# Seven products for half of the first expert's inner width on two thirds of the tokens

## The chip, the cores and the metric

One core of a Trainium2 chip runs the whole program in one launch. The time is the device time of one execution in microseconds (us), as a median over runs. The engines are TensorE (PE, with its weight loads as PEld), VectorE (DVE), ScalarE (ACT), GpSimd (POOL) and SyncE (SP), which issues nearly all DMAs.

## What is computed

Three layers follow each other on 2304 tokens of width 512. Attention of the linear kind comes first, then a mixture of four experts with dense gates, then a two-layer network with an ELU:

```python
# 4 batches x 8 heads, 576 tokens, head width 64
q_s = exp(q - max_d q); q_s /= sum_d q_s
k_s = exp(k - max_s k); k_s /= sum_s k_s
x = q_s @ (k_s^T @ v)                     # -> 2304 tokens x 512
p = probs / probs.sum(-1)
y = sum over e in 0..3 of p[:, e] * (relu(x @ w1[e]) @ w2[e])     # inner width 1024 each
h = y @ w_in                              # inner width 2048, weights in float64
out = where(h > 0, h, exp(min(h, 0)) - 1) @ w_out
```

## The kernel before

**Number format.** Each float32 operand of a matmul is kept as two parts, a high one rounded for the PE and a low one (the rest). A product then takes three matmuls: high by high, low by high, high by low. Every value that PE writes therefore costs one ACT instruction (the high part) and one DVE or POOL instruction (the low part).

**Plain stage.** Expert 0 goes by plain products. The tokens are cut into `blocks`: seven of 256 and one of 512. The inner width of 1024 is cut into 8 parts of 128 (`FPU = 8`, index f). For every (block, f) `first` calls `hidden` (12 matmuls: 4 of depth by 3), has ACT write the relu's high part (L1440) and DVE its low part (L1441), and then `second` does the 12 matmuls of the (block, f) before this one (L1408 does all plain matmuls). So the order on PE is hidden(k), second(k-1), hidden(k+1), second(k).

**Seven products.** All later work goes in steps (s, b): s counts slices of 4 parts (512) of inner width, b the three groups of 768 tokens. Both layers of a step are a 2 by 2 block product that is done by seven products instead of eight (`PRODUCTS`, `SECOND`), with sums and differences of the quarters made beforehand on DVE and POOL. A step has 84 matmuls of 384 columns for the first layer (L1578) and 84 for the second (L1788 in the experts, L1701 in the last network), which are done in between the products of the next step. The slice s = `S_MOE` is the first of the last network: there the tokens are the experts' sums, and their quarters are split on the spot (`own_steps`, L1346 and L1354).

**Side work.** While PE does the plain stage, the other engines prepare what comes later. `at(n, fn)` hangs a piece of work on hook n; a hook falls due after every 2048 columns of plain matmuls (`HOOK`), which is 24 hooks for a block of 256 tokens with 8 parts. Hung there are:

- the attention of the 12 pairs of heads whose tokens come later (`plan_k`, `plan_q`; names like `qmax`, `ksub`, `kvlo`, with L564, L579, L485, L610, L632, L552, L462 on DVE). Batch i / 4 must be done before the block that holds its first token.
- `spread(b)` for the three groups of tokens: the sums T1 to T4 of the quarters of x and their two parts, L953 (two inputs in SBUF, 128 x 768) and L959 (low part), each on DVE or on POOL as the table `MOVES` says, then stored to DRAM for the seven products.
- eight of the 32 pieces of `convert`, which turn the float64 weights of the last network into float32 with integer operations on DVE (L710, L716, L720, L726, L729). The other 24 lie in the steps.
- the gates (`normalise`, `p_turn`, `p_scale` with L903) and the weights of the first step (`w1_steps`).

In the steps `at2` does the same with 24 hooks a step. `MOVES` holds some hundreds of numbers that shift single pieces from their hook or name their engine (`'d'` DVE, `'p'` POOL). Each engine works through its instructions in the order in which they were written down; nothing is reordered on the chip.

## Time and profile before

| | |
|---|---|
| median of 3 runs | 1157.36 us (1156.95 to 1158.04) |
| the profiled execution | 1158.24 us, of which the span of its instructions is 1156.5 us |
| PE busy | 1139.9 us, 99% |
| DVE busy | 959.2 us, 83% |
| POOL busy | 665.2 us, 58% |
| ACT busy | 655.7 us, 57% |
| HBM | 230 GB/s over the span |

The profile comes from one execution. Busy time of an engine is the time in which at least one of its instructions is under way. A matmul's shown duration includes its way through the array, so PE counts as busy also where the next matmul starts long before the last has ended; how fast PE goes is read from the distance of the starts.

### The profile page before, as it was taken

Reading aid. Unit: us, or ns where it says so; the run is one execution under the profiler, and the core shown is the slowest. Engines: PE = TensorE matmul, PEld = TensorE weight load, DVE = VectorE, ACT = ScalarE, POOL = GpSimd, SP = SyncE. Lnnn points to the kernel's source line nnn. Section 1 sums busy time; section 2 is a strip of 40 time slices with the busy share of each in tenths; the row PEclk is TensorE's granted clock in tenths of the full one; section 3 lists DMA queues with packets and bytes.
Section 4 is the critical chain, followed back from the end, with each engine's and each line's share of the span. In section 5 each row is a group of like instructions: output and inputs, shape, how many; then the busy total and the mean of one; then the engine's idle time right before and its main releaser. Section 6 shows DMA issues by size and latency. Waiting matters only on the chain. (4 is left out here: it accounts for less than half of the span.)

```text
span 1156.5 us, 20274 instructions
## 1 busy us (share of the span) xinstructions
PE 1139.9 (99%) x7198; PEld 1117.8 (97%) x7198; DVE 959.2 (83%) x1538; ACT 655.7 (57%) x1386; POOL 665.2 (58%) x567
## 2 busy tenths in 40 slices
PE   8999999999999999999999999999899999999998
PEld 7999999989999999999999999998899999999998
DVE  8977877766788888899899988989787979879976
ACT  6554543335455455455445445456798767767763
POOL 4523445326567567567666655666687547645643
PEclk9999999999999999999999999999999999999999
DMA  9556555876677776777877887814777564665463
GB/s 275 151 144 215 176 193 191 308 251 250 246 255 264 271 261 257 271 269 262 284 274 241 303 266 259 284 68 159 275 242 266 200 231 173 230 230 205 174 247 109
DMA packets 125241, 266.77 MB, mean 231 GB/s; under 512 B 12428, under 2 KB 50004, under 8 KB 125140
## 3 DMA queue, kind: packets, MB, share of 16 engines
q1 hardware_dynamic: 122900, 262.33, 65.6%
q10 hardware_dynamic: 2240, 3.15, 0.8%
q8 instruction: 57, 0.93, 0.3%
q14 instruction: 44, 0.36, 0.1%
HBM read 218.21 MB, written 47.22 MB: 230 GB/s over the span
## 5 line engine op out<-in xcount | busy, mean ns | idle before, releaser
L1578 PE MATMUL m<-xh,w1s 128*128 128x384 f32 x840 | 245.0, 337 | 5.5 <-DVE half L1632 2.9
L1578 PE MATMUL h<-xh,w1s 128*128 128x384 f32 x840 | 243.7, 336 | 1.8 <-DVE half L1632 1.1
L1578 PEld LDWEIGHTS m<-xh,w1s 128*128 128x128 f32 x840 | 154.3, 188 | 9.9 <-DVE half L1632 3.2
L1578 PEld LDWEIGHTS h<-xh,w1s 128*128 128x128 f32 x840 | 154.3, 188 | 5.1 <-DVE m L1871 1.8
L1578 PE MATMUL m<-xl,w1s 128*128 128x384 f32 x420 | 140.7, 335 | 0.0
L1578 PE MATMUL h<-xl,w1s 128*128 128x384 f32 x420 | 140.4, 334 | 0.0
L1408 PE MATMUL o<-hpa,w2t 128*128 128x256 f32 (+1 forms) x768 | 119.3, 300 | 1.0 <-DVE hpa L1441 0.8
L1408 PE MATMUL h<-xh,w1t 128*128 128x256 f32 (+1 forms) x512 | 111.3, 296 | 0.0
L1408 PEld LDWEIGHTS o<-hpa,w2t 128*128 128x128 f32 x768 | 103.9, 191 | 5.7 <-DVE hpa L1441 1.4
L1816 POOL TENSOR_TENSOR accs<-part,accs 128x768 f32<-128x768 f32 x35 | 67.6, 1932 | 68.8 <-DVE part L1815 60.9
L1788 PE MATMUL o<-xh,w2g 128*128 128x384 f32 x432 | 95.2, 334 | 0.0
L1788 PE MATMUL o<-hpa,w2g 128*128 128x384 f32 x432 | 93.7, 334 | 0.0
L1788 PE MATMUL o<-xl,w2g 128*128 128x384 f32 x432 | 93.4, 335 | 0.0
L1408 PEld LDWEIGHTS h<-xh,w1t 128*128 128x128 f32 x512 | 85.6, 191 | 2.5
L1121 POOL TENSOR_TENSOR w2g<-r,w2g 128x512 fp32r<-128x512 f32 x56 | 80.9, 1453 | 12.2 <-ACT w2g L1120 12.2
L1578 PEld LDWEIGHTS m<-xl,w1s 128*128 128x128 f32 x420 | 78.9, 188 | 0.2
L1578 PEld LDWEIGHTS h<-xl,w1s 128*128 128x128 f32 x420 | 78.9, 188 | 0.0
L1408 PE MATMUL h<-xl,w1t 128*128 128x256 f32 (+1 forms) x256 | 77.0, 301 | 0.5 <-DVE xl L632 0.5
L1788 PEld LDWEIGHTS o<-xl,w2g 128*128 128x128 f32 x432 | 76.4, 188 | 0.5 <-ACT o L1798 0.3
L1788 PEld LDWEIGHTS o<-xh,w2g 128*128 128x128 f32 x432 | 76.6, 188 | 0.1
L1788 PEld LDWEIGHTS o<-hpa,w2g 128*128 128x128 f32 x432 | 76.6, 188 | 0.0
L1714 DVE TENSOR_TENSOR accs<-o,accs 128x768 f32<-128x768 f32 (+1 forms) x69 | 62.6, 908 | 4.3 <-PE o L1701 4.3
(366 smaller groups left out, 2899.6 us busy)
## 6 DMA issues: line engine op xcount, KB each, us to landing
xh<-xs SPq DMA_DIRECT2D x189, 384.0 KB, 6.1
xl<-xs SPq DMA_DIRECT2D x189, 384.0 KB, 6.5
xs<-xh SPq DMA_DIRECT2D x42, 384.0 KB, 3.9
xs<-xl SPq DMA_DIRECT2D x42, 384.0 KB, 4.0
r<-in_w_dram SPq DMA_DIRECT2D x56, 256.0 KB, 3.9
extra<-prow SPq DMA_DIRECT2D x38, 192.0 KB, 5.8
x<-in_w_in_dram SPq DMA_DIRECT2D x12, 512.0 KB, 5.1
x<-in_w_out_dram SPq DMA_DIRECT2D x12, 512.0 KB, 6.1
```

What stands on the lines that cost most here:

```text
L1121: eng_of(nc.gpsimd, "w2lo", cls(s), op).tensor_tensor(out=t[:, 1], in0=src, in1=t[:, 0].bitcast(F32), op=ALU.subtract)
L1408: nc.tensor.matmul(out, lhsT, rhs, **kw)
L1578: nc.tensor.matmul(dst, t[:, wl, c + dl, :], x[xl_][:, dl, :], start=(n == 0 and p < 2), stop=(n == 5), skip_group_check=True,)
L1714: nc.vector.tensor_tensor(out=a, in0=x, in1=a, op=ALU.add)
L1788: nc.tensor.matmul(o[:, m], l, r, start=(k < 2 and n == 0), stop=(n == 5), skip_group_check=True)
L1816: nc.gpsimd.tensor_tensor(out=a, in0=r, in1=a, op=ALU.add)
```

## The change

Expert 0's inner width is halved by way of doing it: f = 0 to 3 stay plain for all tokens. f = 4 to 7 stay plain for the first three blocks (`FULL = 3`, 768 tokens) only; for the tokens from 768 on they become a new slice s = 0 of the seven products, with the steps (0, 1) and (0, 2) (`STEP0 = 1` leaves out the step (0, 0)). All later slices move up by one. The plain stage has 144 hooks instead of 216, so the attention of the last 12 pairs starts in a closer rhythm (`K_START`: every 7 hooks instead of every 11), the three `spread` start 20 and 26 hooks apart and go one piece a hook (36 apart and one piece every second hook before), the gates go early, and six of the eight conversions of the plain stage go into the steps (six for each spell of three steps in the second and third spell, instead of four). `spread` keeps its running sums in `gt` instead of a pool's tile, and puts T1 to T4 into other quarters. The table `MOVES` has new numbers nearly throughout, by which also single sums and low parts change between DVE and POOL.

```diff
@@ -22,209 +22,267 @@
...
+    ('spe', 1, 1): 'd', ('spe', 1, 10): 'd', ('spe', 1, 12): 'd', ('spe', 1, 13): 'p',
...
@@ -275,7 +333,7 @@
-    K_START = [8, 13, 20, 29] + [40 + 11 * n for n in range(8)]
+    K_START = [8, 13, 20, 29] + [38 + 7 * n for n in range(8)]
...
-    STEPS = [(s, b) for s in range((NU - 1) * FPU // FS) for b in range(NB)]
-    S_MOE = (E - 1) * FPU // FS
+    STEPS = [(s, b) for s in range((NU * FPU - FS) // FS) for b in range(NB)]
+    STEP0 = 1
+    FULL = 2 * TB // 256
+    S_MOE = (E * FPU - FS) // FS
...
         def new(n):
-            r = stg.tile([P, 2, DM], F32, tag="r", name="sum")
-            t[n] = r[:, :, :TB]
+            k = "ab".index(n)
+            t[n] = gt[:, 2 * k : 2 * k + 2]
...
-            u, c = divmod(FPU + s * FS + f, FPU)
+            u, c = divmod(FS + s * FS + f, FPU)
...
     for b in range(NB):
         need = min(NP_, -(-2 * TB * (b + 1) // S) * NPAIR)
-        t = 66 + 36 * b
+        t = (66, 86, 112)[b]
...
-            at(t + 2 * n, grd(b, n, fn, need), "sprd", b, n)
...
+            at(t + n * (1, 1, 1)[b], grd(b, n, fn, need), "sprd", b, n)
...
-    CONV = [(at, t, 1 + (t < 100), True) for t in (30, 50, 70, 146, 160, 173, 185, 197)]
+    CONV = [(at, t, 1 + (t < 100), True) for t in (30, 50)]
     SPELL = NB * SH
     CONV += [
         (later, SPELL * n + t, d, False)
         for n in range(S_FAST)
-        for t, d in (((10, 2), (34, 1), (48, 1), (62, 1)) if n < 3 else ((6, 1), (20, 1), (34, 1), (48, 1), (62, 1)))
-        if (n, t) != (0, 10)
+        for t, d in (((59, 1),) if n == 0 else ((20, 1), (34, 1), (48, 1), (62, 1)) if n == 5 else
+                     ((6, 1), (18, 1), (30, 1), (42, 1), (54, 1), (66, 1)) if n < 3 else
+                     ((6, 1), (20, 1), (34, 1), (48, 1), (62, 1)))
     ]
...
+    def parts_in(bi):
+        return FPU if bi < FULL else FS
+
     def hidden(u, bi, fs, d0, d1):
...
-    steps = [(0, bi, (f,)) for bi in range(len(blocks[0])) for f in range(FPU)]
+    steps = [(0, bi, (f,)) for bi in range(len(blocks[0])) for f in range(parts_in(bi))]
...
     for i, (s, b) in enumerate(STEPS):
         moe, fill = s < S_MOE, {}
-        if fast(i - 1):
+        if i < STEP0:
+            continue
+        if i == STEP0:
+            pass
+        elif fast(i - 1):
```

How the order of instructions moves is shown at three places. The first is PE in the fourth block of the plain stage (tokens 768 to 1023), where f = 3 ends; the numbers of the weights' buffers tell the parts apart. Before, w1t_449 is f = 3 and w1t_504 is f = 4:

```order
L1408 MATMUL h_1711<-xh_89,w1t_449 128x256
L1408 MATMUL o_1653<-hpa_92,w2t_433 128x256 x6
L1408 MATMUL o_1654<-hpa_92,w2t_433 128x256 x2
...
L525 MATMUL m_1748<-accs_91,ek_1600 64x65 x10
L1408 MATMUL o_1654<-hpa_92,w2t_433 128x256 x4
L1408 MATMUL h_1772<-xh_89,w1t_504 128x256
```

In the changed kernel w1t_326 is f = 3 and w1t_320 is f = 0:

```order
L1491 MATMUL h_1834<-xh_89,w1t_326 128x256
L1491 MATMUL o_1752<-hpa_92,w2t_325 128x256 x6
L1491 MATMUL o_1753<-hpa_92,w2t_325 128x256 x2
...
L655 MATMUL m_1870<-ident_81,accs_91 128x96 x6
L539 MATMUL m_1878<-gx0_93 128x128
L1491 MATMUL o_1753<-hpa_92,w2t_325 128x256 x4
L1491 MATMUL h_1888<-xh_89,w1t_320 128x256
```

After f = 3 the next block begins, where f = 4 followed.

The second place is DVE between two relus of that stage (L1441 before, L1527 in the changed kernel, the same instruction). Before, from the 28th relu to the 29th and on:

```order
L1441 SCALAR_TENSOR_TENSOR hpa<-h,hpa 128x256
L953 TENSOR_TENSOR sum<-sum,xl 128x2x384
L564 TENSOR_REDUCE qm<-accs 96x12
L1441 SCALAR_TENSOR_TENSOR hpa<-h,hpa 128x256
L485 TENSOR_TENSOR ek<-m,ek 128x640
L610 TENSOR_TENSOR ql<-m,qh 128x576
L726 SCALAR_TENSOR_TENSOR ce<-gt,ce 128x512
L1441 SCALAR_TENSOR_TENSOR hpa<-h,hpa 128x256
```

In the changed kernel, in the block of tokens 1024 to 1279 (L1027 is L953, L1033 is L959, L692 is L632, L630 is L570, L612 is L552):

```order
L1527 SCALAR_TENSOR_TENSOR hpa<-h,hpa 128x256
L692 TENSOR_TENSOR xl<-m,xh 128x576
L1027 TENSOR_TENSOR gt<-xh 128x768
L554 TENSOR_SCALAR ks<-m 128x1
L555 RECIPROCAL ks<-ks 128x1
L1027 TENSOR_TENSOR gt<-gt,xl 128x768
L630 TENSOR_TENSOR accs<-accs,qm 96x768
L612 SCALAR_TENSOR_TENSOR kvs<-m,ks,kvs 64x64 x2
L1527 SCALAR_TENSOR_TENSOR hpa<-h,hpa 128x256
```

Where two or three larger instructions stood between two relus, five stand now.

The third place is POOL in the same stretch. Before (L587 and L570 are the two products and differences on q, L474 a memset):

```order
L953 TENSOR_TENSOR sum<-xh 128x2x384
L474 MEMSET gx_93 128x128
L570 TENSOR_TENSOR accs<-accs,qm 96x768
L953 TENSOR_TENSOR sum<-sum,xl 128x2x384
L587 TENSOR_TENSOR accs<-accs,qs 96x768
L474 MEMSET accs 128x128
L959 TENSOR_TENSOR xl<-sum,xh 128x2x384
```

In the changed kernel (L647 is L587):

```order
L647 TENSOR_TENSOR accs<-accs,qs 96x768
L534 MEMSET accs 128x128
L1027 TENSOR_TENSOR gt<-gt,xl 128x768
L1027 TENSOR_TENSOR gt<-xh,gt 128x768
L1027 TENSOR_TENSOR gt<-gt,xl 128x768
L534 MEMSET gx0_93 128x128
L1033 TENSOR_TENSOR xl<-gt,xh 128x2x384
L1027 TENSOR_TENSOR gt<-xh,gt 128x768
L1027 TENSOR_TENSOR gt<-gt,xl 128x768
L1033 TENSOR_TENSOR xl<-gt,xh 128x2x384
```

The pieces of `spread` stand closer to each other here, with fewer pieces of the attention between them.

## Rows read from the trace of the kernel before

**Rows 1.** The page: busy time of each engine.

```profile
PE 1139.9 (99%) x7198; PEld 1117.8 (97%) x7198; DVE 959.2 (83%) x1538; ACT 655.7 (57%) x1386; POOL 665.2 (58%) x567
```

**Rows 2.** Stretches: length, busy PE, PEld, DVE, ACT, POOL (instructions), granted clock, DMA.

```profile
40.00:222.00 182.00, 181.96 (x1662) 178.44 (x1661) 139.61 (x253) 84.62 (x175) 71.64 (x52) 1.00 0.61 198
343.00:600.00 257.00, 256.89 (x1476) 255.28 (x1476) 222.68 (x327) 128.57 (x267) 169.92 (x131) 1.00 0.77 267
774.00:815.00 41.00, 34.20 (x184) 31.34 (x183) 39.03 (x59) 29.49 (x59) 29.25 (x23) 1.00 0.40 149
```

**Rows 3.** Timeline of PE: first and last of a hidden's twelve matmuls, twice.

```profile
102.28 0.28 PE L1408 MATMUL h<-xh,w1t 128*128 128x256 f32 x1
...
103.60 0.28 PE L1408 MATMUL h<-xh,w1t 128*128 128x256 f32 x1
...
252.94 0.39 PE L1408 MATMUL h<-xh,w1t 128*128 128x512 f32 x1
...
255.44 0.39 PE L1408 MATMUL h<-xh,w1t 128*128 128x512 f32 x1
```

**Rows 4.** The chain that ended last, one piece: start, length, what.

```profile
848.33 2.08 PE o L1701 x12
```

**Rows 5.** Groups on DVE from 40 to 222 us: busy, mean ns, idle before.

```profile
L1441 DVE SCALAR_TENSOR_TENSOR hpa<-h,hpa 128x256 fp32r<-128x256 f32 x51 | 21.3, 418 | 20.8 <-ACT hpa L1440 20.5
L953 DVE TENSOR_TENSOR sum<-sum,xl 128x768 f32<-128x768 f32 x8 | 12.8, 1596 | 1.1 <-POOL sum L953 1.0
L579 DVE TENSOR_REDUCE qs<-accs 96x12 f32<-96x768 f32 x12 | 11.2, 937 | 1.0 <-ACT accs L574 0.9
L564 DVE TENSOR_REDUCE qm<-accs 96x12 f32<-96x768 f32 x11 | 10.3, 941 | 0.0
...
L632 DVE TENSOR_TENSOR xl<-m,xh 128x576 fp32r<-128x576 f32 x12 | 9.0, 753 | 6.1 <-ACT xh L628 5.9
...
L959 DVE TENSOR_TENSOR xl<-sum,xh 128x768 fp32r<-128x768 f32 x7 | 6.6, 945 | 1.3 <-ACT xh L956 1.2
L720 DVE SCALAR_TENSOR_TENSOR gt<-gt 128x512 f32<-128x512 uint32 x5 | 5.8, 1166 | 0.0
...
L462 DVE TENSOR_REDUCE nm<-gx 128x1 f32<-128x576 f32 x6 | 4.5, 742 | 0.0
L953 DVE TENSOR_TENSOR sum<-xh,sum 128x768 f32<-128x768 f32 x4 | 3.8, 947 | 0.0
...
L953 DVE TENSOR_TENSOR sum<-xh 128x768 f32<-128x768 f32 x3 | 2.8, 947 | 0.0
...
L710 DVE TENSOR_SCALAR ce<-gt 128x512 uint16<-128x512 uint16 x5 | 2.7, 538 | 1.4 <-DMA gt<-in_w_in_dram 1.4
```

**Rows 6.** Instructions by line: least, median and longest ns, first and last start.

```profile
L1441 DVE SCALAR_TENSOR_TENSOR hpa<-h,hpa x64: 357/423/693, 24.4 to 256.6; 128x256 fp32r<-128x256 f32 x56, 128x512 fp32r<-128x512 f32 x8
...
L903 DVE TENSOR_TENSOR accs<-accs,gx x6: 681/950/2597, 224.2 to 254.3; 128x768 f32<-128x768 f32 x5, 128x512 f32<-128x512 f32 x1
```

**Rows 7.** Timeline of DVE, then of POOL, around 174 us.

```profile
174.09 4.02 DVE L953 TENSOR_TENSOR sum<-sum,xl 128x768 f32<-128x768 f32 x1 [1.03 <-POOL sum L953]
178.03 0.41 DVE L1441 SCALAR_TENSOR_TENSOR hpa<-h,hpa 128x256 fp32r<-128x256 f32 x1
...
174.02 1.47 POOL L570 TENSOR_TENSOR accs<-accs,qm 96x768 f32<-96x768 f32 x1
175.45 1.84 POOL L959 TENSOR_TENSOR xl<-sum,xh 128x768 fp32r<-128x768 f32 x1
```

**Rows 8.** Groups on ACT and on POOL from 40 to 222 us.

```profile
L1440 ACT ACTIVATE hpa<-h 128x256 fp32r<-128x256 f32 x51 | 19.4, 380 | 45.6 <-PE h L1408 45.5
...
L953 POOL TENSOR_TENSOR sum<-sum,xl 128x768 f32<-128x768 f32 x10 | 18.6, 1858 | 9.9 <-DVE sum L953 9.6
```

**Rows 9.** PE's longest wait, and the stretch right behind it.

```profile
PE m L1578 <- DVE half L1632: 2.9, 1, 2.9
815.00:826.00 11.00, 11.00 (x57) 11.00 (x56) 6.91 (x10) 7.08 (x15) 5.94 (x5) 0.85 0.74 288
```

125 lines of the change are left out of this document (75 added, 50 removed), and 439 rows, old and new, of the table MOVES.

## The prediction

> **What bounds the kernel now.** The page comes first: PE is busy for 99% of the span, the next engine, DVE, for 83% [rows 1]. A share of 99% does not say how fast PE goes, so the next view is PE's timeline, and there the distance of the starts. In the plain stage the twelve matmuls of a hidden start from 102.28 to 103.60, eleven distances in 1.32 us, 0.120 us for 256 columns; with 512 columns it is 2.50 / 11 = 0.227 us [rows 3]. In the steps the chain shows twelve matmuls of 384 columns in 2.08 us, 0.1733 us each [rows 4]. PE goes at these rates nearly everywhere. The table of stretches gives the exception: from 774 to 815 us, where the slice S_MOE begins, it is idle for 6.8 of 41 us and DVE busy for 39.0 [rows 2]. So time is PE's work, plus the places where DVE can't keep up. In the plain stage it could: 139.6 of 182 us, with PE idle for 0.04 us [rows 2].
>
> **The change, PE's part.** Removed are f = 4 to 7 of blocks 3 to 7 (counted from 0). Four blocks of 256 lose 4 x 4 x 24 = 384 matmuls, 384 x 0.120 = 46.1 us; the block of 512 loses 96, x 0.227 = 21.8 us. Added are two steps of 168 matmuls, 336 x 0.1733 = 58.2 us. PE's work falls by 46.1 + 21.8 - 58.2 = **9.7 us**. The seam between plain stage and first step is the same in both orders, so it costs nothing new.
>
> The rows give 32 columns' worth more per matmul than its own columns at 2.4 GHz (0.120 against 0.107 us), for each size. The Trainium skill, TensorE: Matmul & The Clock Gate, section Back-to-back issue gap, gives a lone matmul N/2.4 + 2.5 ns; by it the three prices would be 0.109, 0.216 and 0.163 us and the gain 8.0 us, as an estimate. The trace's rates differ from it, and the sum goes by the trace.
>
> **DVE in the shorter plain stage.** The attention of 12 pairs and the three spreads have 72 hooks less to hide under. I counted DVE's instructions in the changed order by blocks. The densest are blocks 3 and 4 (tokens 768 to 1279, eight relus): 8 L1441 at 0.418, 5 L953 at 1.293 (the mean over its three rows, (8 x 1.596 + 7 x 0.947) / 15), 4 L959 at 0.945, and three each of L579, L564, L485, L632, L610 and L462, 4.93 us for the six [rows 5]. That is 3.3 + 6.5 + 3.8 + 14.8 = 28.4 us. Another 26 instructions (2 L903 at 0.950 [rows 6], 3 L570, 1 L587, 8 L552 and 12 small ones of the same view) make 10.1 us. Instructions that follow at once overlap: the relu of 178.03 starts 0.08 us before the one of 174.09 ends [rows 7]; 61 x 0.08 = 4.9 us. DVE needs 38.5 - 4.9 = **33.6 us** there.
>
> PE needs 8 x 24 x 0.120 = 23.0 us for the plain work, and the attention of three pairs. From the first relu to the last are 232.2 us [rows 6], of which plain matmuls take about 198 (1344 x 0.120 + 192 x 0.227, less a hidden and two seconds at the ends). The other 34 us are the 12 pairs, the second halves of the first four and the waits at the start; I take 2.3 us a pair. PE: 23.0 + 6.9 = **29.9 us**. DVE is short by 3.7 us on these rows. In the two blocks before it is about even (31 us of each by the same count), in the two after it needs some 2 us less than PE.
>
> The rows flatter it. At 174.09 an L953 with a normal time of 0.95 us takes 4.02: POOL works on L570 and then L959 without a gap, ending at 177.29, and DVE ends 0.82 us later [rows 7]. A DVE instruction with all its operands in SBUF waits for POOL here; one that reads PSUM (L632, mean 0.753) shows nothing of the kind, nor do the reductions (L579, L564) [rows 5]. The Trainium skill says this in SBUF — State Buffer, section Who interferes with whom: with two inputs in SBUF a DVE instruction contends with POOL's reads and the second to start is blocked. By this rule the trace agrees (3.07 us lost in that one row), and the change brings more of both: it speaks against the change.
>
> Its price: over the L953, L959, L570 and L587 of rows 5's view (27 instructions with two SBUF inputs) the lost time is 8 x 0.65 = 5.2 us, 0.19 each, with POOL busy for 71.6 of 182 us, 39% [rows 2]. In blocks 3 and 4 POOL has 20.8 us of work in 29.9 (7 L953 at 1.858 [rows 8], the rest two L959, two L587 and three memsets), 70%. Scaled, 0.19 x 70 / 39 = 0.35 us for 15 such instructions: 5.2 us. Without any loss DVE needs 33.6 - 1.7 = 31.9 us, with this loss **37.1 us**. Bounds: 31.9 us, if none is held; and 15 x 0.7 x 0.93 (half an L953 of POOL) = 9.8 us more, 41.7 us, if each meets POOL at random. I take 37.1, since the row that it is nearest to is the same instruction in the same stage.
>
> **What of the lag PE sees.** A relu's low part is first read by the third matmul of its second, after second(k-1) and hidden(k+1): 26 x 0.120 = 3.1 us behind its hidden. ACT's 0.38 [rows 8] and its own 0.42 go off, so DVE may be 2.3 us late. Queued behind a late relu on DVE is the rest of the attention, for which PE's next kv and x matmuls wait, so the lag does not leave PE by another way. PE's wait: 37.1 - 29.9 - 2.3 = **4.9 us**; 0 at the lower bound, 9.5 at the upper.
>
> **The six conversions.** They cost some 4.4 us each on DVE (0.538 for L710 to 1.166 for L720, five instructions [rows 5]) and go to spells of 87 us, which hold six instead of four or five. From 343 to 600 us DVE is busy for 87% and PE lost 0.1 of 257 us [rows 2]; 5 points more should cost little. I take 0.5 us, 0 to 3. The gates and weights placed anew cost nothing under the same cover, and if it goes, they are in the count above.
>
> **Sum.** -9.7 + 4.9 + 0.5 = -4.3 us. The profiled execution took 1158.24 us, 1.7 more than its span and 0.9 more than the median; what lies around the span stays, so the difference goes onto the median: 1157.36 - 4.3 = **1153.1 us**. A measurement here tells about 0.2% (2.3 us) from no change.
>
> **Rivals.**
>
> - *The whole gain.* The lag stays under 2.3 us, because few DVE instructions meet POOL: 1157.4 - 9.7 = 1147.7 us, with some of the conversions 1149. For it: seven of fifteen L953 lost nothing [rows 5]. Against: even without loss DVE is 2 us short.
> - *All given back to POOL.* The upper bound, 9.5 us, and 1 to 3 for the conversions: 1158 us, from 1156 to 1161. For it: POOL at 70% where DVE has no slack. Against: 0.19 us a piece before, where chance at 39% would have given 0.39 x 0.93 = 0.36. The rule of SBUF — State Buffer in the Trainium skill, quoted above, is the mechanism of this rival; the trace bears it out, but at half that price.
> - *Slower, by the first step's parts.* Step (0, 1) reads its sums from DRAM. Its last two loads now go out about 8 hooks (7.7 us) before it, where 28 lay between, and its loads overwrite quarters in which the last spread's sums lie until these are stored. If POOL or DVE delays that store by more than PE is delayed, PE waits in one piece. After its longest wait, 2.9 us, PE went 11 us at a mean clock of 0.85 (the level of 1.2 GHz for a part of it), 1.65 us lost [rows 9]; so 8 us in one piece cost 9.7, with the 4.9 above: 1162 us. It decides from about 7 us on. Against: the hooks are counted in PE's columns and slip with PE, and the two late loads serve the last two products of seven.
> - *S_MOE.* Its DVE work is not changed, only its order; the 6.8 us lost there [rows 2] may shrink or grow by some 4: 1149 or 1157.
>
> **How the numbers follow.** Forecast 0.46 (own range 1150.5 to 1156); whole gain 0.22; given back 0.16; a late part 0.06; S_MOE 0.05 each way. Faster by over 0.2%, below 1155.0: 0.22 + 0.05 + four fifths of 0.46, 0.64. Slower, above 1159.7: 0.06 and under half of the 0.16, 0.13. Same: the rest, 0.23. The range leaves a third of the whole gain's cases below, and above it the late part and a third of the cases that give all back: 1148 to 1160.
>
> **What would show it.** Right: 84 x 32 = 2688 matmuls in the place of L1578, and 960 of 256 columns and 96 of 512 in that of L1408 (1344 and 192 before); in the stretch of blocks 3 and 4 DVE busy over 95%, PE with waits for L1441's or L632's place of 3 to 7 us in total, and L953's rows on DVE with a mean above 1.3 us. Wrong: DVE under 90% there with PE unbroken (the whole gain), or PE's longest wait at the seam for a DMA (the late part), or a change of more than 3 us between the waits near S_MOE.

## The result, and the profile after

The changed kernel takes 1167.19 us (median of 4, 1164.67 to 1167.59), the kernel before beside it 1157.15 (1155.97 to 1158.04): ratio 1.0083 [1.0065, 1.0100]. It is slower by some 10 us, where 1153.1 was forecast and 1148 to 1160 as the range. The profiled execution of after has a span of 1165.6 us, 9.1 above that of before.

The page of after, busy time of each engine, against [rows 1]:

```profile
PE 1137.4 (98%) x7054; PEld 1115.0 (96%) x7054; DVE 993.6 (85%) x1607; ACT 677.0 (58%) x1428; POOL 677.5 (58%) x578
```

PE has 144 matmuls fewer and its busy time fell by 2.5 us only; the span grew. Stretches of after, columns as in [rows 2]:

```profile
35.00:39.00 4.00, 3.75 (x31) 3.75 (x32) 3.93 (x11) 0.98 (x3) 1.39 (x2) 1.00 0.40 132
41.00:46.00 5.00, 2.48 (x17) 2.30 (x16) 4.16 (x4) 1.58 (x4) 2.58 (x3) 0.86 0.01 3
45.00:49.00 4.00, 4.00 (x23) 4.00 (x24) 3.37 (x6) 2.55 (x6) 2.57 (x3) 0.63 0.30 80
...
50.00:200.00 150.00, 144.71 (x1291) 137.51 (x1292) 129.75 (x231) 78.17 (x158) 72.74 (x52) 1.00 0.77 245
120.00:150.00 30.00, 27.22 (x263) 25.90 (x263) 29.03 (x53) 18.60 (x36) 21.13 (x13) 1.00 0.90 284
325.00:450.00 125.00, 121.88 (x690) 118.76 (x689) 111.02 (x178) 63.56 (x133) 71.01 (x58) 1.00 0.77 260
792.00:806.00 14.00, 13.29 (x68) 12.96 (x66) 12.18 (x18) 10.52 (x21) 11.08 (x8) 0.88 0.43 141
```

From 120 to 150 us, in the dense blocks of the plain stage, DVE is busy for 29.0 of 30 us and PE idle for 2.8; over 150 us of that stage PE is idle for 5.3 (0.04 of 182 us before [rows 2]). From 325 to 450 us it is idle for 3.1 of 125, at a mean DVE share of only 89%; there [rows 2] had 0.1 of 257. PE's waits in after, as in [rows 9]:

```profile
PE o L1877 <- DVE o L1889: 2.9, 2, 1.5
PE o L1491 <- DVE hpa L1527: 2.5, 2, 2.1
PE m L539 <- issue: 2.5, 1, 2.5
PE m L1667 <- DVE half L1721: 2.4, 1, 2.4
PE m L1667 <- DVE xl L1437: 2.4, 1, 2.4
```

Only the last two belong to S_MOE. The second and third lie at 33 and 42 us, the first at 328 and 418. For the third the profile names no releaser; L539 starts 0.11 us behind the end of DVE's L692 at 44.75 (below). Idle time misses what PE loses at a low clock, so I summed, over all matmuls, the distance of each start to the next less the median distance of its line and shape. That is PE's lost time, in us, by stretches of the span, for every kernel of this study (the labels are those of the experiments). Waits given below without their line are such distances, some 0.15 us above the idle time that the profile gives:

```
                0-50 50-200 200-325 325-450 450-775 775-850 rest   sum
before           9.6    5.0     0.7     0.6     4.0    11.0   1.7   32.4
after           15.0   12.0     1.7     6.0     2.8    10.7   2.1   50.3
e1               9.0   11.6     3.5     4.4     2.9     9.8   2.3   43.4
b4              12.4    5.2     0.7     0.6     3.9     9.3   1.3   33.5
e2              12.3   12.0     2.0    12.0     2.9     7.1   2.7   51.0
e4              14.9   12.5     1.8     5.2     2.6     7.1   2.4   46.5
e9               9.0   12.5     2.5     4.8     2.6     7.2   2.3   41.0
e10              9.1   10.9     3.2     4.1     7.2     9.5   2.3   46.4
e11             10.8   13.2     5.1     0.9     2.9     8.5   2.4   43.8
e14              9.2   12.0     8.6     0.9     2.9     9.5   2.6   45.6
b3               9.3    5.1     0.7     0.6     5.3     9.5   2.2   32.7
e3              12.1   10.4     3.4     4.9     3.2     7.2   1.9   43.2
e5              15.0   15.7     2.3     6.1     2.6     9.5   2.1   53.3
e6              12.1   13.6     2.1     6.3     2.6     8.4   2.6   47.7
e7              15.0   11.0     2.3     6.3     3.0    10.6   2.5   50.8
e8              12.2    7.4     4.2     4.4     2.5     8.5   2.1   41.4
e12              8.1    8.5     5.6     0.9     3.4     9.4   2.0   38.0
e13              9.1    9.4     3.2     4.2     3.1     9.5   2.0   40.5
e15              8.2    8.6     8.5     0.9     3.1     8.5   2.0   39.9
e16              8.8    9.3     1.4     0.9     7.9     6.0   2.5   36.9
```

The edges of the stretches stand still while the kernels get shorter: the second spell's wait, at 327.5 us in after, comes before 325 in e1, e3 and e8 (in e9, e10 and e13 the first of two) and counts there under 200 to 325. To compare the spells, the two columns from 200 to 450 us have to be added.

After lost 17.9 us more than before: 5.4 in the start (0 to 50 us), 7.0 in the plain stage, 5.4 in the steps of the second and third spell (325 to 450), 0.1 in all the rest. The median distances are what they were (0.120, 0.227 and 0.173 us), and the counts are those forecast (2688, 960, 96), so PE's work did fall by 9.7. 17.9 - 9.7 = 8.2 of the 9.1 us by which the span grew. The 0.9 left over lie in the method: the 24 matmuls of L539 (L479 before) come in pairs with distances of 0.113 and 0.028 us, and the median falls on 0.070 before and on 0.110 after, which hides 1.0 us.

**The start.** Timeline of after, DVE, then POOL (start, length, engine, line):

```profile
27.69 0.55 DVE L647 TENSOR_TENSOR accs<-accs 96x384 f32<-96x384 f32 x1
...
31.85 3.02 DVE L647 TENSOR_TENSOR accs<-accs 96x384 f32<-96x384 f32 x1
34.79 0.41 DVE L1527 SCALAR_TENSOR_TENSOR hpa<-h,hpa 128x256 fp32r<-128x256 f32 x1
...
39.61 4.78 DVE L630 TENSOR_TENSOR accs<-accs,qm 96x768 f32<-96x768 f32 x1
44.31 0.44 DVE L692 TENSOR_TENSOR xl<-m,xh 128x288 fp32r<-128x288 f32 x1
...
31.94 1.29 POOL L735 TENSOR_TENSOR w1t<-r,w1t 128x512 fp32r<-128x512 f32 x1
33.19 1.26 POOL L735 TENSOR_TENSOR w2t<-r,w2t 128x512 fp32r<-128x512 f32 x1
...
39.66 1.30 POOL L735 TENSOR_TENSOR w2t<-r,w2t 128x512 fp32r<-128x512 f32 x1
40.91 0.21 POOL L534 MEMSET accs<- 128x128 f32 x1
41.07 1.29 POOL L735 TENSOR_TENSOR w1t<-gt,w1t 128x512 fp32r<-128x512 f32 x1
42.32 1.26 POOL L735 TENSOR_TENSOR w2t<-gt,w2t 128x512 fp32r<-128x512 f32 x1
```

L647 takes 0.55 us at 27.69 and 3.02 at 31.85; it ends 0.42 us behind POOL's second L735. L630 (median 0.948) takes 4.78 and ends 0.81 us behind POOL's last. Right behind each stands what PE waits for, the relu's low part at 34.79 and L692 at 44.31. L735 is the weights' low part, which the new table moved to POOL here. It is the hold of [rows 7], but longer: it lasts through a whole row of POOL's instructions. The Trainium skill, SBUF — State Buffer, section Who interferes with whom, has the loser blocked until the other instruction is done; here L630 waited out three sums of 1.3 us and a memset, and the measurement decides.

**The steps.** Timeline of after, DVE, then POOL, in the second spell (the same stands at 412 to 419 us in the third); L772 to L788 are the conversion, here the fifth of six:

```profile
321.71 0.96 DVE L1904 TENSOR_TENSOR part<-o,extra 128x768 f32<-128x768 f32 x1
322.58 0.42 DVE L772 TENSOR_SCALAR ce<-x 128x512 uint16<-128x512 uint16 x1
322.92 2.06 DVE L778 TENSOR_SCALAR y<-x 128x512 int32<-128x512 int32 x1
...
328.32 0.95 DVE L1889 TENSOR_TENSOR o<-o,m 128x768 f32<-128x768 f32 x1
...
322.75 1.94 POOL L1905 TENSOR_TENSOR accs<-part,accs 128x768 f32<-128x768 f32 x1 [2.19 <-DVE part L1904]
```

L778 (median 0.420) is held for 1.64 us behind POOL's L1905, and L1889, for which PE waits, stands six instructions later. L778 has one input in SBUF; the same section of the Trainium skill lists tensor_scalar among the operations that can contend, if its operands meet conditions that stand on another page. The trace agrees that it can: 2.06 us for 0.42.

**The plain stage.** One line of after, DVE, least, median and longest ns of each form (L1027, the spread, L953 before [rows 5]):

```profile
L1027 DVE TENSOR_TENSOR gt<-gt,xl x11: 891/946/959, 122.0 to 193.5; 128x768 f32<-128x768 f32 x11
L1027 DVE TENSOR_TENSOR gt<-xh,gt x4: 892/952/960, 156.3 to 192.0; 128x768 f32<-128x768 f32 x4
L1027 DVE TENSOR_TENSOR gt<-xh x3: 942/946/2181, 121.0 to 176.9; 128x768 f32<-128x768 f32 x3
```

Of 18 one was held, at 176.9 us, and none in blocks 3 and 4, where the forecast put the holds. There it is POOL that loses. DVE, then POOL:

```profile
122.83 0.95 DVE L630 TENSOR_TENSOR accs<-accs,qm 96x768 f32<-96x768 f32 x1
...
122.99 2.48 POOL L1027 TENSOR_TENSOR gt<-gt,xl 128x768 f32<-128x768 f32 x1 [2.85 <-DVE gt L1027]
...
129.17 1.86 POOL L1027 TENSOR_TENSOR gt<-gt,xl 128x768 f32<-128x768 f32 x1
```

POOL's L1027 begins 0.16 us behind DVE's L630 and takes 2.48 us for 1.86. At 126.65, 134.68 and 145.93 it likewise begins while DVE is in such an instruction, and takes 2.41 to 2.49. At these four places DVE had started first and kept its time, 0.95 to 1.05 us. PE's longest waits from 50 to 200 us:

```profile
PE m L655 <- issue: 1.4, 3, 0.7
PE m L539 <- DVE xl L692: 1.0, 1, 1.0
PE m L679 <- DVE ql L670: 1.0, 2, 0.7
```

They stand ahead of the attention's matmuls; no wait of this stretch is put down to a relu (L1527).

### The profile page after: what moved, and what is told of

Same layout as the page of the kernel before. It is cut to its first block, busy times and chain, and to the rows that moved or that the text cites. A ratio compares the mean times of both kernels' runs of the same rounds, so it can differ in the third digit from the quotient of the medians.

```text
span 1165.6 us, 20156 instructions
## 1 busy us (share of the span) xinstructions
PE 1137.4 (98%) x7054; PEld 1115.0 (96%) x7054; DVE 993.6 (85%) x1607; ACT 677.0 (58%) x1428; POOL 677.5 (58%) x578
## 5 line engine op out<-in xcount | busy, mean ns | idle before, releaser
L1667 PE MATMUL m<-xh,w1s 128*128 128x384 f32 x896 | 262.1, 337 | 2.4 <-DVE half L1721 2.4
L1667 PE MATMUL h<-xh,w1s 128*128 128x384 f32 x896 | 259.5, 335 | 2.2 <-DVE half L1721 1.3
L1905 POOL TENSOR_TENSOR accs<-part,accs 128x768 f32<-128x768 f32 x38 | 72.3, 1902 | 70.4 <-DVE part L1904 67.0
L1877 PE MATMUL o<-xh,w2g 128*128 128x384 f32 x480 | 107.0, 336 | 0.0
L1877 PE MATMUL o<-xl,w2g 128*128 128x384 f32 x480 | 104.4, 335 | 0.3 <-DVE o L1898 0.2
L1198 POOL TENSOR_TENSOR w2g<-r,w2g 128x512 fp32r<-128x512 f32 x50 | 69.2, 1386 | 34.7 <-ACT w2g L1197 34.7
L1491 PE MATMUL o<-hpa,w2t 128*128 128x256 f32 (+1 forms) x528 | 83.2, 300 | 2.7 <-DVE hpa L1527 2.5
L1491 PEld LDWEIGHTS o<-hpa,w2t 128*128 128x128 f32 x528 | 71.9, 194 | 5.7 <-DVE hpa L1527 3.3
L1491 PE MATMUL h<-xh,w1t 128*128 128x256 f32 (+1 forms) x352 | 75.1, 292 | 0.0
L1691 POOL TENSOR_TENSOR hpa<-gt,hpa 128x384 fp32r<-128x384 f32 x30 | 30.6, 1019 | 56.9 <-ACT hpa L1689 56.9
L1491 PEld LDWEIGHTS h<-xh,w1t 128*128 128x128 f32 x352 | 58.5, 191 | 1.3
```

What stands on the lines that cost most here:

```text
L1198: eng_of(nc.gpsimd, "w2lo", cls(s), op).tensor_tensor(out=t[:, 1], in0=src, in1=t[:, 0].bitcast(F32), op=ALU.subtract)
L1491: nc.tensor.matmul(out, lhsT, rhs, **kw)
L1667: nc.tensor.matmul(dst, t[:, wl, c + dl, :], x[xl_][:, dl, :], start=(n == 0 and p < 2), stop=(n == 5), skip_group_check=True,)
L1691: eng.tensor_tensor(out=gl, in0=g, in1=gh.bitcast(F32), op=ALU.subtract)
L1877: nc.tensor.matmul(o[:, m], l, r, start=(k < 2 and n == 0), stop=(n == 5), skip_group_check=True)
L1905: nc.gpsimd.tensor_tensor(out=a, in0=r, in1=a, op=ALU.add)
```

## The experiments

The kernels of one line of thought stand together. Ratios are against the kernel before on the same chip, with 95% intervals.

**e1, the start.** Two of q's pieces from DVE to POOL:

```diff
-    ('qmul', 2, 1): 'd', ('qsub', 4, 0): 'd',
+    ('qmul', 2, 1): 'p', ('qsub', 4, 0): 'p',
```

> The changed kernel with two DVE instructions of the start given to POOL: the product on q of the pair 2, second half (L647, at 31.85 us, 3.02 us long where the same form took 0.55 at 27.69), and the difference on q of pair 4 (L630, at 39.61 us, 4.78 long where 0.94 is normal). Nothing else moves. Theory 'held': both stood on DVE until POOL's row of low parts of weights ended (2.5 and 3.8 us), and PE's two longest waits behind them (2.1 us at 33 for L1527, 2.5 us at 42) and the lower clock after the second (0.83 in 40 to 50 us) are their price; they vanish and the time falls by 4 to 6 us, to 1161 to 1163. Theory 'load': DVE has simply too much work in the start; then two instructions of 1.5 us in all are worth at most 1.5 us, POOL's queue gets 2.3 us longer, and the time is 1165.5 to 1168.

Measured 1162.73 us, 1.0032 [1.0022, 1.0043]. The start lost 9.0 us instead of 15.0 (before 9.6), both waits gone. The start's price is that of two DVE instructions beside a row on POOL.

**b4, the same in the kernel before.** Before, with after's engines for the first weights and q's pieces, 12 entries like

```diff
-    ('wlo', 0, 1): 'd', ('wlo', 5, 0): 'd', ('wlo', 5, 1): 'd', ('wlo', 7, 1): 'd',
+    ('wlo', 0, 1): 'p', ('wlo', 5, 0): 'p', ('wlo', 5, 1): 'p', ('wlo', 7, 1): 'p',
+    ('qmul', 1, 1): 'd', ('qsub', 4, 0): 'd',
```

> The kernel before with the changed kernel's choice of DVE or POOL in the start: the low parts of the plain weights, and the products and differences on q of the pairs 0 to 4, by the twelve entries in which the tables differ there. Nothing else of the change. Theory 'held': what costs 4.8 us in the changed kernel is that POOL gets a long row of low parts just where DVE gets instructions on SBUF; the same choice costs the kernel before 3 to 5 us, 1161 to 1163. Theory 'place': it takes the new places of the pieces as well, and the choice alone costs less than 1.5 us, 1157 to 1159.5.

Measured 1160.91 us, 1.0030 [1.0020, 1.0039]. Timeline of b4, DVE (L592 is L647 of after, L587 of before):

```profile
31.87 3.01 DVE L592 TENSOR_TENSOR accs<-accs 96x384 f32<-96x384 f32 x1
```

The same instruction is held for the same time in a kernel that otherwise is the one before, at a cost of 0.3%. The choice of engines is enough for the first wait, without the shorter plain stage. It is not the whole price: the start lost 12.4 us here, 2.8 more than in before, where after lost 5.4 more. The difference on q is held too (3.42 us at 41.02), but PE's wait of 2.7 us at 42 does not come; that one needs after's order of instructions as well.

**e2, the fifth conversion earlier.** Its pieces come some hooks forward in the second and third spell:

```diff
-    ('cl', 1054): 3.953, ('c', 1042, 6): 4.988, ('c', 1054, 0): 0.538, ('c', 1054, 1): -0.115,
+    ('cl', 1054): 2.6, ('c', 1042, 6): 4.1, ('c', 1054, 0): -0.6, ('c', 1054, 1): -1.3,
```

> The changed kernel with the first two instructions of one conversion in each of the two spells that hold six (L772 and L778, at 321.7 and 412.2 us) about one hook earlier, ahead of the sum L1904 that releases POOL's L1905. The work is the same, six conversions stay in each spell. Theory 'held': L778 (2.06 us where 0.41 is normal) stands behind POOL's L1905, so L1889 and with it PE's second layer come 1.6 us late, once in each spell; moved ahead, both waits of 1.5 us go, the time falls by 3 to 4 us, to 1163 to 1164.5. Theory 'load': six conversions are too many for a spell wherever they stand; PE's wait comes up at another place of the spell and the time is 1166.5 to 1168.

Measured 1168.72 us, 1.0096 [1.0080, 1.0112]. Timeline of e2, DVE:

```profile
317.93 0.43 DVE L772 TENSOR_SCALAR ce<-x 128x512 uint16<-128x512 uint16 x1 [2.14 <-DMA x<-in_w_out_dram]
318.94 0.43 DVE L778 TENSOR_SCALAR y<-x 128x512 int32<-128x512 int32 x1 [0.57 <-DMA scratch<-y]
...
323.17 1.50 DVE L1851 TENSOR_TENSOR gt<-gt 128x384 f32<-128x384 f32 x1
324.60 1.50 DVE L1151 TENSOR_TENSOR w1s<-r,w1s 128x512 fp32r<-128x512 f32 x1
326.02 1.48 DVE L782 SCALAR_TENSOR_TENSOR y<-x,y 128x512 f32<-128x512 uint32 x1
```

L778 is no longer held, and nothing is won: DVE first waits 2.7 us for two DMAs, and then three instructions that took 0.55 to 1.25 us in after take 1.5 each beside POOL. PE waits 3.2 us in each spell where it waited 1.64.

**e4, the fifth conversion later.**

```diff
-    ('c', 1054, 0): 0.538, ('c', 1054, 1): -0.115, ('c', 1054, 2): 0.764, ...
+    ('c', 1054, 0): 4.2, ('c', 1054, 1): 3.3, ('c', 1054, 2): 2.9, ...
```

> The changed kernel with the fifth conversion of the two spells that hold six moved the other way: its first three instructions (L772, L778, L782) stand behind L1889 and the two instructions after it, so that none of the three is between L1904 and L1889, and nothing waits on DVE for the load of its numbers ahead of L1889 (in the run that moved them earlier DVE stood 2.1 and 0.6 us for DMAs there, which gave PE 3.2 us of wait for 1.6). Theory 'held' as refined by that run: L1889 comes 2.5 to 3 us earlier (L778 2.06, L782 0.68 and the overlap off), PE's two waits of 1.6 us before the second layer go, and nothing else is late; the time falls by 3 to 4 us, to 1163 to 1164.5 beside 1167.5 for the changed kernel. Theory 'load': six conversions are too many for a spell; the wait turns up at another DVE place of the spell and the time stays at 1166.5 to 1168.

Measured 1163.46 us, 1.0051 [1.0037, 1.0065]. In the steps two waits of 0.67 and 0.69 us took the place of each 1.64: 0.8 us less from 325 to 450. Another 3.6 us less were lost from 775 to 850, where nothing was moved (see the last section). So the held instruction is not what the six conversions cost; moved away, they cost nearly as much. The time lies in the range of the theory 'held', but by luck: the waits that this theory had going did not go.

**e9, the start and the fifth conversion.** The edits of e1 and of e4.

```diff
+    ('qmul', 2, 1): 'p', ('qsub', 4, 0): 'p',
+    ('c', 1054, 0): 4.2, ('c', 1054, 1): 3.3, ('c', 1054, 2): 2.9, ...
```

> The changed kernel with the two repairs that each helped alone: the two DVE instructions of the start given to POOL (1.0032 of the time before, alone) and the fifth conversion behind L1889 (1.0051 alone; the changed kernel 1.0083). If the two are independent, as their places 290 us apart say, the differences add: 1.0083 - 0.0051 - 0.0032 = 1.0000 of the time before, 1157 us. If most of the second one's gain was the clock after the waits of the slice S_MOE (in that run's profile PE lost 6.8 us from 775 to 850, in the changed kernel's 10.3, with no instruction of that stretch moved) and not its own place (0.9 us in the profile), then 1160 to 1162.

Measured 1159.38 us, 1.0018 [1.0008, 1.0029]. By time the two do not add up in full: that would have been 1.0000. The profile, which caught the fastest of the twelve executions (1157.95 us), has both gains, 9.0 us lost in the start and 7.3 from 200 to 450; what is left over before are the plain stage and the spells.

**e10, both conversions out of the plain stage as well.** e9, and:

```diff
-    CONV = [(at, t, 1 + (t < 100), True) for t in (30, 50)]
+    CONV = []
...
-                     ((6, 1), (18, 1), (30, 1), (42, 1), (54, 1), (66, 1)) if n < 3 else
+                     ((6, 1), (18, 1), (30, 1), (42, 1), (54, 1), (66, 1)) if n < 5 else
...
```

> The run before this one, and the last two conversions of the plain stage (at hooks 30 and 50) moved into the fourth and fifth spell, which then hold six too. DVE's work from 66 to 112 us falls by 5.4 us (L772, L778, L782, L788, L791, twice), with two loads and two stores. Theory 'DVE': PE's loss from 50 to 125 us, 6.0 in the changed kernel, falls by 2 to 3, and 1 comes back in the two spells: 1 to 2 us under the run before. Theory 'rhythm': the waits of that stretch stay, 1 us is lost in the spells: 0 to 1.5 us over it.

Measured 1163.56 us, 1.0048 [1.0036, 1.0060]. The plain stage lost 10.9 instead of 12.5, but the fourth and fifth spell, which now hold six as well, have the two waits (0.67 and 0.6 to 0.73) too: from 450 to 775 us 7.2 instead of 2.6. A sixth conversion cost PE time in each of the four spells where it was tried.

**e11, five in every spell.** e1, and:

```diff
-        for t, d in (((59, 1),) if n == 0 else ((20, 1), (34, 1), (48, 1), (62, 1)) if n == 5 else
-                     ((6, 1), (18, 1), (30, 1), (42, 1), (54, 1), (66, 1)) if n < 3 else
+        for t, d in (((48, 1), (62, 1)) if n == 0 else
...
```

> The changed kernel with the start repaired (the two DVE instructions given to POOL) and five conversions in each of the spells 2 to 6, two in the first: no spell holds six. The moved conversions stand at the places that other spells of five have. Theory 'six': the waits in the two spells (two of 1.6 us, or two pairs of 0.7 after the fifth was moved) come from twelve hooks being too few for a conversion, whatever its place; with fourteen they go, without a new one: 3 to 4 us under the run with the start alone (1.0032 of the time before), 0.9995 to 1.001. Theory 'place': each conversion that stands between L1904 and L1889, or right behind, costs, in a spell of five too; some of the 3 us come up again: 1.002 to 1.0035.

Measured 1161.2 us, 1.0030 [1.0019, 1.0041]. From 325 to 450 us 0.9 us are lost, as before the change (0.6): six in a spell is the cause of that term. But the first spell got two, and from 200 to 325 us 5.1 are lost. Timeline of e11, DVE:

```profile
225.23 0.43 DVE L772 TENSOR_SCALAR ce<-x 128x512 uint16<-128x512 uint16 x1 [3.54 <-DMA x<-in_w_in_dram]
```

DVE waits 3.5 us for the conversion's load, and PE then 2.2 us for what stands behind it (L1962).

**e14, the first spell's two later.** e11 with

```diff
-        for t, d in (((48, 1), (62, 1)) if n == 0 else
+        for t, d in (((53, 1), (65, 1)) if n == 0 else
...
```

> The run with five in every spell and the start repaired, with the two conversions of the first spell at hooks 53 and 65 in place of 48 and 62. There, DVE stood 4.1 us for the load of the first of them, which waited for the second layer's low parts to let go of the buffer that it shares, and PE waited 2.4 to 3.1 us behind it and lost 1.4 more at the lower clock. Theory: with the load five hooks later it finds the buffer free, DVE does not wait, and the 3.7 us go: 1157 to 1158.5, 0.9995 to 1.0007 of the time before. Rival: the SP queue still stops at that load and the seven products' loads stand behind it, or DVE waits at the new place: 1.002 to 1.003 as before.

Measured 1163.34 us, 1.0050 [1.0038, 1.0062]. From 200 to 325 us 8.6 us are lost, more than in e11. Timeline of e14, DVE:

```profile
228.20 0.42 DVE L778 TENSOR_SCALAR y<-x 128x512 int32<-128x512 int32 x1
228.65 2.21 DVE L782 SCALAR_TENSOR_TENSOR y<-x,y 128x512 f32<-128x512 uint32 x1
```

DVE still waits 1.9 us for the load (L772 at 223.56), and now L782 (0.68 in after) is held as well. PE waits at 233, 247 and 265 us, 1.9, 1.3 and 2.2.

**e3, without q's maximum.** DVE and POOL work taken out of the dense stage, on after as it is. The exponentials are then taken of q itself, which gives the same quotient only as long as none of them overflows:

```diff
     def q_max(i, ps, halves):
+        if i >= NPAIR:
+            return
...
     def q_sub(i, ps, halves):
+        if i >= NPAIR:
+            return
```

> The changed kernel without the maximum of q and its subtraction (L624, L630) for the twelve later pairs; the exponentials are taken of q itself, and the quotient is the same but for rounding. DVE loses twelve reductions of 0.94 us and seven of the twelve differences (0.95), POOL the other five (1.47). Theory 'load' (the prediction's own): from 75 to 175 us DVE's work is longer than PE's, and PE's 10.8 us of lost time there (3.9 in the kernel before) is what DVE lacks; with some 15 us less on DVE over that stretch the loss falls to 3 to 5, the held L630 at 39.61 goes as well (2.5 us of wait and the clock after it, some 4), and the time is 1155 to 1159. Theory 'chain': PE waits for the length of the attention's chains through ACT, DMA and PE, which only get 2 us shorter; the loss from 75 to 175 stays above 8, and the time is 1161 to 1164, by the start alone.

Measured 1161.52 us, 1.0035 [1.0022, 1.0047]. Stretches of e3:

```profile
50.00:200.00 150.00, 146.23 (x1275) 139.83 (x1274) 113.52 (x211) 78.66 (x158) 67.55 (x51) 0.99 0.78 250
120.00:150.00 30.00, 28.21 (x261) 27.31 (x261) 24.13 (x46) 17.20 (x33) 20.76 (x13) 0.94 0.86 284
```

DVE has 16.2 us less to do in the plain stage, and is busy for 24 of 30 us in its densest part; PE's loss fell by 1.6 of the 7.0 us only. Timeline of e3, DVE:

```profile
114.71 0.82 DVE L545 TENSOR_TENSOR ek<-m,ek 128x640 f32<-128x640 f32 x1 [1.87 <-DMA ek<-in_kn_dram]
...
131.13 0.75 DVE L522 TENSOR_REDUCE nm<-accs 128x1 f32<-128x576 f32 x1 [0.99 <-DMA accs<-in_k_dram]
```

DVE, no longer late, waits for the loads of k instead, and PE 1.79 us at 132.9 behind the second of them. SP's own wait shows why that one came late (line waited at, releaser: us in total, times, longest):

```profile
SPq L1024 <- DVE xl L1037: 3.6, 1, 3.6
```

SP stood for 3.6 us at a store of the spread (L1024), for DVE's L1037 at 126.39; the load of k behind it went out at 127.81 and landed after 3.3 us, where 3.4 is the median of the loads of k. The load waited for at 114.71, of the second copy of k, had another reason: it went out at 108.90 and took 5.7 us, where 3.8 is the median of its kind, while the DMA engines were busy for 88% (108 to 116 us). What SP's order and what slow transfers cost in all was not told apart.

**b3, the same in the kernel before.**

```diff
+        if i >= NPAIR:
+            return
```

> The kernel before without the maximum of q and its subtraction (L564, L570) for the twelve later pairs, as a control of the run before this one. Theory 'load': DVE was no bound in the plain stage there (PE idle for 0.04 us from 40 to 222 us), so the same 15 us of DVE work are worth nothing but the small excess of 1 us per 25: 1155.5 to 1157.5. Theory 'chain': shorter chains help the kernel before by as much as the changed one, 2 to 4 us.

Measured 1158.15 us, 0.9998 [0.9989, 1.0006]. Where DVE is not short, this work is worth nothing, so versions without it may be set against before.

**e5, the second copy of k loaded first.**

```diff
-            if i + 2 < NP_:
-                at(kt["kv"] + .01, lambda i=i: load(i + 2, "kv"), "kq", i, "kv")
             if i + 1 < NP_:
-                at(kt["kv"] + .02, lambda i=i: load(i + 1, "n"), "kq", i, "kv")
+                at(kt["kv"] + .01, lambda i=i: load(i + 1, "n"), "kq", i, "kv")
+            if i + 2 < NP_:
+                at(kt["kv"] + .02, lambda i=i: load(i + 2, "kv"), "kq", i, "kv")
```

> The changed kernel with one load in another place: the load of kn for the next pair goes out ahead of the loads of k and v for the pair after it, where it stood behind them. Nothing else changes on any engine. Theory 'chain': PE's kv matmuls of one pair let the one buffer of kn go, then come the load (4.0 us in the middle, up to 6.1), L545, ACT's exponential and the next pair's kv matmuls; with pairs every 7 hooks this ring is as long as the rhythm, so a load that starts 1.3 to 2 us earlier takes off 1 to 3 us, to 1164.5 to 1166.5. Theory 'load': DVE's work sets the end there, the load's wait was hidden behind it; 1167 to 1168.

Measured 1170.25 us, 1.0101 [1.0085, 1.0118]; the plain stage lost 15.7. SP's waits from 50 to 165 us, the longest in total, first of after, where it is at the load of v (L509):

```profile
SPq L509 <- PE m L585: 26.6, 9, 4.9
```

and of e5, where it is at the load of the second copy of k (L498):

```profile
SPq L498 <- PE m L585: 47.4, 10, 15.6
```

SP stands for up to 15.6 us at a load whose buffer PE has not yet let go, and the loads of k and v behind it, whose place may be free, stand too. The loads wait for buffers, in SP's order.

**e6, both.** The edits of e3 and of e5.

```diff
+        if i >= NPAIR:
+            return
...
+                at(kt["kv"] + .01, lambda i=i: load(i + 1, "n"), "kq", i, "kv")
```

> The changed kernel without the maximum of q and its subtraction for the twelve later pairs, and with the load of kn first. Without the maximum alone the loss from 50 to 200 us was 10.4 us, where the run with the same start had 12.0 and the kernel before 5.1; DVE then waited for kn (1.9 us) and k (1.0 us) at the two largest of PE's waits (1.5 and 1.95 us, after which PE ran 18 matmuls at the lower clock, 1.6 us). Theory 'two bounds': DVE's work and the ring of the kn load are both too long, each hides the other, and taking both away brings the loss to 5 to 7: 1157 to 1159.5 beside 1161.5. Theory 'rhythm': PE's waits come from the seven hooks themselves, whatever the load's place, and the time stays within 1 us of 1161.5.

Measured 1165.05 us, 1.0064 [1.0052, 1.0076]; the plain stage lost 13.6, with one wait of 3.1 at 132.6. Less work on DVE does not make up for the worse order of loads.

**e7, without ten pairs' loads.** The loads of q, k, both copies, and v are left out for the pairs 6 to 15, which work on what lies in the buffers:

```diff
         for w in parts:
+            if i >= NPAIR + 2:
+                if w == "n":
+                    st["ek", i] = st["ek"]
+                continue
```

> The changed kernel without the loads of q, k, kn and v for the pairs 6 to 15: these pairs work on what lies in the buffers. All work of PE, DVE, ACT and POOL stays; 50 DMAs are left out, some 12 MB. The loss of PE from 50 to 200 us was 12.0 us in the changed kernel and 5.1 in the one before. Theory 'DMA': the loads, with the spreads' stores beside them (DMA engines busy for 0.90 of 120 to 150 us, 0.69 before), set the pace of the pairs; without them the loss falls to 6 to 8 and the time by 4 to 6 us, to 1161.5 to 1163.5. Theory 'DVE': DVE's own work is too long there, and the loss stays above 10.5, the time within 1.5 us of 1167.2.

Measured 1166.71 us, 1.0065 [1.0045, 1.0085]; the plain stage lost 11.0, 1.0 less. The loads alone are not it either.

**e8, neither loads nor maximum.** The edits of e3 and of e7.

```diff
+            if i >= NPAIR + 2:
...
     def q_max(i, ps, halves):
+        if i >= NPAIR:
+            return
```

> Both left out of the changed kernel: the loads for the pairs 6 to 15, and the maximum of q and its subtraction for the twelve later pairs. Theory 'two bounds': DVE's work and the loads each hold the pairs up when the other is gone, so that only both together bring the loss from 50 to 200 us to 5 to 7 us, the level of the kernel before (the maximum alone: 10.4); the time is 1155.5 to 1158, beside 1161.5 without the maximum alone. Theory 'rhythm': PE's waits follow from pairs that come every seven hooks (the second is to start when PE and ACT have ended the first), whatever DVE and the DMAs do: the loss stays at 9 to 10.5 and the time at 1160 to 1162.

Measured 1157.71 us, 0.9999 [0.9990, 1.0007]. Stretches of e8:

```profile
50.00:200.00 150.00, 148.03 (x1291) 141.29 (x1291) 117.17 (x214) 79.10 (x160) 67.34 (x51) 1.00 0.50 175
```

The plain stage lost 7.4: 4.6 of the 7.0 us are gone, where either alone gave 1.6 and 1.0. By time, too, leaving out the loads is worth more once the maximum is gone: 0.36% (e3 to e8, intervals apart) against 0.18% (after to e7, intervals that overlap). DVE's work and the loads bound this stage one right behind the other. The last 2.4 us stay unexplained.

**e12, e13 and e15: e11, e9 and e14 without the maximum.** All three take e3's edit on top:

```diff
     def q_max(i, ps, halves):
+        if i >= NPAIR:
+            return
```

> The run before this one, and no maximum of q and its subtraction for the twelve later pairs (the quotient is the same but for rounding). In the kernel before that was worth nothing (0.9998). If DVE's work is one of the two bounds of the plain stage (without the maximum alone 1.6 us less in the profile, and lower clock after its waits), this is 1.5 to 3 us under the run before it, 0.997 to 0.999 of the kernel before: the first version under it. If its gain came only from the held L630 of the start, which the repair has taken away already, there is no gain over the run before.

> Start repaired, fifth conversion behind L1889 (together 1.0018 of the time before), and no maximum of q for the later pairs. Same question as the run before this one, with the other repair of the spells: theory 'DVE in the plain stage': 1.5 to 3 us less than 1.0018, 0.9992 to 1.0005; else 1.0018. Beside the run with five in every spell it says what the two pairs of 0.7 us that are left in the spells cost: 2 to 3 us.

> The run before this one without the maximum of q for the twelve later pairs. Theory: the same 3.7 us off 0.9993 of the time before: 0.9955 to 0.9972, 1152.5 to 1154.5, clear of both kernels. Rival as in the run before this one: 0.9985 to 1.0.

Measured 1156.72 us, 0.9993 [0.9984, 1.0002]; 1156.61, 0.9995 [0.9986, 1.0003]; 1157.12, 1.0003 [0.9988, 1.0018]. None is apart from before. In the plain stage the five kernels that have no maximum but do have the loads in the old order (e3, e12, e13, e15, e16) lost 8.5 to 10.4 us, the seven with it (after, e1, e2, e4, e9, e11, e14) 11.6 to 13.2: by the means, 9.2 and 12.2, the maximum is worth some 3 us there, more than e3's own 1.6. Beside 3.0 and 1.0 the 4.6 of e8 is little more than the sum: what shows the loads as a bound of their own is e3's rows and these five kernels' 9.2 against 7.4 without loads, not the excess. The first spell lost 5.6 and 8.5 us in e12 and e15, so its waits do not hang on the maximum.

**e16, the sixth conversions after the spells.** e1 and e3, one conversion in the first spell, five in each other, and one more behind the spells:

```diff
-        for t, d in (((59, 1),) if n == 0 else ((20, 1), (34, 1), (48, 1), (62, 1)) if n == 5 else
-                     ((6, 1), (18, 1), (30, 1), (42, 1), (54, 1), (66, 1)) if n < 3 else
+        for t, d in (((59, 1),) if n == 0 else
...
-    CONV += [(later, end1 + t, 1, False) for t in (11, 22, 33)]
+    CONV += [(later, end1 + t, 1, False) for t in (11, 22, 33, 57)]
```

> Start repaired, no maximum of q for the later pairs, five conversions in each of the spells 2 to 6, the first spell's one where the changed kernel has it, and the one that is left over at hook 57 of the slice ahead of S_MOE, where DVE is busy for 44 of 50 us. Theory: no spell gets a new wait, so the 3.1 us of wait and 1.4 of lower clock of the run with two in the first spell go: 0.9993 less 0.0039, 0.995 to 0.997 of the kernel before, 1152 to 1154.5. Rival: DVE has no room there either and hands the delay to the slice S_MOE, which waits for DVE at its start: 0.9985 to 1.001.

Measured 1153.7 us (1151.84 to 1154.46), 0.9965 [0.9951, 0.9978], against 1157.46. Stretch of e16:

```profile
325.00:450.00 125.00, 125.00 (x720) 124.12 (x719) 108.94 (x171) 63.96 (x133) 77.28 (x60) 1.00 0.81 274
```

From 325 to 450 us PE is never idle, and DVE is busy for only 2.1 us less than in after. Two waits, of 0.8 and 2.4 us, appear at 758 and 765, where the sixth spell now has a fifth conversion, and the start of S_MOE lost 6.0 where the other kernels lost 7.1 to 11.0. From 450 to 850 us together it lost 13.9, after 13.5, so the sixth conversions were not free there: what e16 gains on after lies ahead of 450 us. This is the first version clear of both kernels. With the maximum it would be some 3 us slower by the means above, 1156.7, which could not be told from before; it was not run.

## Why the prediction was wrong, step by step

- **PE's work, -9.7 us: right.** Counts and distances are those forecast, and e16 shows that part of the gain can be had.
- **DVE short in blocks 3 and 4: right. PE's wait there: mis-sized, for a reason that was not the one given.** DVE is busy for 97% from 120 to 150 us and PE waits. The term was 4.9 us and measured 7.0 over the plain stage, 2.8 of idle time in those 30 us. The sum rested on holds of 0.35 us for 15 instructions on DVE; in blocks 3 and 4 no L1027 was held on DVE; at the four places above DVE had started first and POOL lost the time. Two of the signs failed with it: the waits put down to L632's place (L692) come to 1.5 us from 50 to 200 and those to L1441's (L1527) to none, not 3 to 7 in all, and the mean of L1027 on DVE was 1.01 us, not above 1.3. In the place of the holds stands a second bound, the loads of k, which come late by SP's order (e3, e5) and in part by slow transfers (e3): 1.6 us back without part of DVE's work (3 by the means), 1.0 without the loads, 4.6 without both. The count of DVE's needs against PE's could not have shown it, since no term spoke of a load of the plain stage.
- **The six conversions, "5 points more should cost little. I take 0.5 us, 0 to 3": this step failed.** They cost 5.4 us. With five in the second and third spell 0.9 is lost from 325 to 450 us (e11, e12, e14, e15, e16). With six, from 200 to 450 us, 7.0 to 7.7 are lost wherever the fifth stands (after, e4, e9, e10), or 14.0 (e2), against 2.3 in e16. The reading was off as well: these two spells get two conversions more each, at the sum's own price 8.8 of 87 us, 10 points and not 5. The mean share of DVE hid it: 89% from 325 to 450 us in after, 87% in e16, which loses nothing. A late piece at one place, behind which PE's next operand is queued, is what a mean over 125 us does not show.
- **"The gates and weights placed anew cost nothing under the same cover, and if it goes, they are in the count above": this step failed.** In the start the new engines put two DVE instructions beside a row on POOL: 5.4 us. Two letters take back 6.0 (e1), and the new engines cost the kernel before 0.3% (b4). I had priced the hold, from [rows 7], for the plain stage alone, and the start not at all.
- **The sum.** -9.7 + 7.0 + 5.4 + 5.4 + 0.1 = +8.2 us, against -4.3. The two steps priced at 0.5 together make 10.3 of the difference of 12.5, the plain stage 2.1.
- **The rivals.** The whole gain did not come. The part that gives all back to POOL had the mechanism but the wrong place, and ended at 1161. The late first step did not come: 200 to 325 us lost 1.7. S_MOE moved by less than its own scatter.

## What to carry to other kernels

A change that empties one engine has to be priced at every place where it moves work between engines that share a path, even far from the stage it is about: two entries of a table cost more here than the whole gain that was forecast. Where a mean share of a side engine is near 90%, look for the instruction that the bottleneck waits for and count what is queued ahead of it, instead of counting points of the share. And if taking out one suspect gives back little, take out two at once before dropping either: the plain stage gave 1.6 to 3, 1.0 and, together, 4.6.
